# Reordering the first loads of a block-sparse attention and bilinear feed-forward kernel

## The chip, the cores and the metric

The kernel runs on one core of one Trainium2 chip. The metric is device time in microseconds (us), from the start of the program to its end, as the median of several runs; lower is better. One execution more is profiled, and all rows below come from that one.

## The reference

Attention over 4 batches, 8 heads, 768 positions and head size 64, with a block mask (24 blocks of 32), followed by a bilinear feed-forward (3072 tokens, 512 to 1536 to 512):

```python
scores = scale * np.matmul(q, k.transpose(0, 1, 3, 2))
mask = np.abs(blk_i - blk_j) <= 1
mask = mask | (blk_i == 0) | (blk_j == 0) | (blk_i == 23) | (blk_j == 23)
for qb in range(24):
    for kb in sampled_blocks[qb]:            # three random blocks a row
        mask[qb*32:(qb+1)*32, kb*32:(kb+1)*32] = True
scores = np.where(mask, scores, -1e9)
attn = np.exp(scores - max); attn = attn / (sum + 1e-9)
x = np.matmul(attn, v)                       # to (B*S, H*D)
out = ((x @ w_a) * (x @ w_b)) @ w_out
```

Each block row attends to at most eight blocks (itself, its neighbours, the first, the last and three sampled ones); block rows 0 and 23 attend to all.

## The kernel before

**Tiling.** A chunk is 256 queries, so there are three chunks per batch and twelve in all. They are worked in the order 1, 2, 0, 3 and so on (`seq`). A chunk has eight block rows, called blocks here and numbered n in working order. For a sparse block, GpSimd (POOL) copies its keys out of `keysT` into `KG` (lines 774 to 782), SP loads its value rows into `VG` (lines 809 to 827), TensorE writes the mask and the scores into the PSUM tile `s` (`all_scores`), VectorE takes the row maximum (line 1151), ScalarE the exponential (line 1161), and after normalizing and transposing (lines 1047 and 1054, or a DMA transpose) TensorE sums the values into `av` (line 1074), from which ScalarE and VectorE make `xT`. Batch 0 keys and the first two chunks' values are used as float32 (`plain`); later ones are split into two float16 parts.

**Weights.** The 36 weight tiles (12 each of w_a, w_b, w_out) come as 64-bit numbers on POOL's DMA queue (`weights`, line 914). VectorE makes float32 of each with three instructions (lines 935, 938, 941), then each is bounded, scaled and split into two float16 halves. The feed-forward's first products (`ab`, line 1422) need these and a whole chunk of `xT`; its second ones (`o`, lines 1525 to 1527) follow.

**Tables.** `make_tables` loads five small arrays: the sampled blocks three times in different layouts, the row offsets `c_rows` and the block table `c_blocks`. From them VectorE makes the address tables (`offs`, `offs_k`, `rows_at`: `starts`, lines 520 to 533) and then the mask rows `mrows` and the selecting matrix `ident` (`doubles`, lines 542 to 558). Every sparse block's scores need `mrows`, and every gather of keys or values needs the address tables.

**The order.** No engine's instruction order is written out by hand. The program is a set of generators ("flows"); a planner in the kernel, run when the program is built, gives each requested step a cost in ns and issues next the one that can begin first by those costs, with the flow's rank as a small weight and as the tie-breaker (lower rank first):

```python
best = min(asked, key=lambda a: (a[0] + weigh[a[3].eng] * a[1], a[1]))
```

Ranks are block numbers: a flow with rank 16 stands with the work of block 16. The planner also models eight DMA completion lanes (`LANES = 8`): a transfer can be issued only when the one eight earlier has landed. Ahead of the real pass it tries 500 random changes of the ranks (fixed seed) and keeps those that bring its own end no later. So each cost and each rank that is changed can change the order of instructions anywhere in the program; on the chip, each engine then works strictly through the order that it was given, waiting by semaphores.

Names that matter below: `make_tables`, `make_eye` (loads the 128 by 128 unit matrix that the transposes use), `queries_plain`, `keys_plain` (four loads, one per two heads, on ScalarE's DMA queue, each started from the one before), `weights`, `bound_values` (batch 0's values, 1.5 MB, on POOL's queue, line 634).

Of the kernel before, what the change touches and what calls it, by code (L numbers as in the profile page):

```python
# [61 lines left out]
LEAD_K, LEAD_V, LEAD_Q, LEAD_X, LEAD_G = 10, 9, 8, -1, 2  # L62
GATE_KV, GATE_Q, GATE_G = 10, 10, 4
EARLY_K, EARLY_V, APART = 21, 14, 2
R_W, R_W_STEP = 16, 0.05
FIRST_W = 3
LATE_W, R_V0 = 9, 8
W_PE, W_DVE, W_ACT, W_POOL, W_SP = 0, 1, 0, 0, 2
# [176 lines left out]
Way = namedtuple("Way", "eng ns fn moved extra", defaults=(0, 0))  # L245
# [6 lines left out]
def dve(ns, fn):  # L252
    return [Way("DVE", ns, fn)]
# [10 lines left out]
def load_way(moved, fn):  # L264

    return [Way("LOAD", 475, fn, moved)]
# [7 lines left out]
def sp(ns, moved, fn):  # L274
    return [Way("SP", ns, fn, moved)]
# [72 lines left out]
def program(nc, plan, pools, q, k, v, sampled_blocks, w_a, w_b, w_out, c_blocks, c_ident, c_rows, out):  # L348
# [27 lines left out]
    def take(tag, bufs):  # L376
        return rings.setdefault(tag, Ring(bufs)).take()
# [109 lines left out]
    def make_tables():  # L487

        box = work.tile([P, DM], F32, tag="st", name="mbox", bufs=ST_BUFS)
        held = yield from take("st", ST_BUFS)  # L490
        row = work.tile([P, DM], F32, tag="st", name="mrow", bufs=ST_BUFS)
        held2 = yield from take("st", ST_BUFS)
        sb = box[:NB, 0 : 2 * NR].bitcast(I32).rearrange("p (a b) -> p a b", b=2)
        cb = box[:NB, 8 : 8 + 5 + NB]
        sv = box[:NB, 40:48]
        eq = box[:NB, 48:56]
        dup = box[:NB, 56:64]
        one = row[0:1, 0 : 2 * NR * NB].bitcast(I32).rearrange("p (a b) -> p a b", b=2)
        clamped = row[0:1, 256 : 256 + NR * NB]
        clamped3 = clamped.rearrange("p (b a) -> p a b", b=NR)  # L500
        seen = box[: NR * BLK, 64 : 64 + 2 * NB].bitcast(I32).rearrange("p (a b) -> p a b", b=2)
        within = box[: NR * BLK, 120:121]
        words = sampled_blocks.bitcast(I32)

        def load():
            nc.sync.dma_start(
                one.rearrange("p (r a) b -> p r (a b)", r=NR),
                words.rearrange("(o r x) a -> o r x a", o=1, x=BLK)[:, :, 0],
            )
            nc.sync.dma_start(  # L510
                sb, words.rearrange("(r x) (a w) -> x a r w", x=BLK, w=2)[0]
            )
            nc.sync.dma_start(seen.rearrange("p a b -> p (a b)"), words)
            nc.sync.dma_start(within, c_rows)
            nc.sync.dma_start(cb, c_blocks)

        yield [Way("SP", 1400, load, 250, 1)]

        def starts():
            nc.vector.tensor_scalar(  # L520
                clamped, one[:, :, 0], 0.0, float(NB - 1), ALU.max, ALU.min
            )
            rows = box[: NR * BLK, 128 : 128 + NB]
            nc.vector.tensor_scalar(
                rows, seen[:, :, 0], 0.0, float(NB - 1), ALU.max, ALU.min
            )
            nc.vector.tensor_scalar(
                rows_at, rows, float(BLK), within, ALU.mult, ALU.add
            )
            nc.vector.tensor_scalar(  # L530
                offs[:, :, :NR], clamped3, float(BLK), None, ALU.mult
            )
            nc.vector.tensor_scalar(
                offs_k[:, :, :NR], clamped3, float(BLK // 2), None, ALU.mult
            )

        t = yield dve(1050, starts)
        tables.fire(t)
        held2.fire(t)

        def doubles():
            nc.vector.tensor_copy(sv[:, 0:5], cb[:, 0:5])
            nc.vector.tensor_scalar(
                sv[:, 5:8], sb[:, :, 0], 0.0, float(NB - 1), ALU.max, ALU.min
            )
            nc.vector.memset(ident, 0.0)
            nc.vector.memset(mrows, 0.0)
            nc.vector.tensor_copy(ident[:NB], cb[:, 5 : 5 + NB])
            nc.vector.memset(dup, 0.0)
            at = (0, 1, 2, 3, 7, 4, 5, 6)  # L550
            for s in range(3, 8):
                nc.vector.tensor_scalar(
                    eq[:, :s], sv[:, :s], sv[:, s : s + 1], MASKED, ALU.is_equal, ALU.mult
                )
                nc.vector.tensor_reduce(
                    dup[:, at[s] : at[s] + 1], eq[:, :s], axis=mybir.AxisListType.X, op=ALU.min
                )
            nc.vector.tensor_copy(mrows[:NB], dup.unsqueeze(2).to_broadcast([NB, 8, BLK]))  # L558

        t = yield dve(2300, doubles)  # L560
        held.fire(t)
        mask_ready.fire(t)


    def make_eye():
        gone = yield from take("hl", HL_BUFS)
        t = yield sp(650, 200, lambda: nc.sync.dma_start(eye, c_ident))
        id_ready.fire(t)
        yield eye_used
        gone.fire(eye_used.at)  # L570
# [21 lines left out]
    def keys_plain(g):  # L592
        t = yield load_way(1500, lambda: nc.scalar.dma_start(keys32[:, g], k[0, g]))
        k_ready[0].fire(t)
        if g + 1 < NG:
            plan.start(keys_plain(g + 1), -LEAD_K)
        else:
            plan.start(queries_plain(seq[1]), order[0, seq[1] * PER] - LEAD_Q)
            plan.start(weights(0), R_W)
# [5 lines left out]
    def queries_plain(cc):  # L605
        u0 = order[0, cc * PER]
        yield from gate(u0 - GATE_Q)
        used = yield from take("QT", QT_BUFS)
        q_used[cc] = used
        QT[cc] = QTs[place[cc] % QT_BUFS]  # L610
        t = QT[cc].rearrange("p a h x -> p (a h x)").bitcast(F32)
        if place[cc] < QT_BUFS:
            nc.gpsimd.memset(t[D:, : H // 2 * CH], 0.0)
            nc.gpsimd.memset(t[:D, H // 2 * CH :], 0.0)

        def load():
            nc.sync.dma_start(t[:D, : H // 2 * CH], q0[cc][:D])
            nc.sync.dma_start(t[D:, H // 2 * CH :], q0[cc][D:])

        t = yield [Way("SP", 1100, load, 1700, 1)]  # L620
        q_ready[cc].fire(t)
        n = place[cc] + 1
        if n == NCH:
            b1, c1 = divmod(seq[n], NCH)
            plan.start(queries(seq[n]), order[b1, c1 * PER] - LEAD_Q)
        elif n > 1:
            plan.start(queries_plain(seq[n]), order[0, seq[n] * PER] - LEAD_Q)
# [37 lines left out]
    def keys(b, g):  # L665
        yield from gate(first_of[b] - (GATE_KV if b < 2 else EARLY_K - APART * g))
        raw, freed = yield from raw_tile(b, g, 0)
        yield pool_load(1000, 1000, lambda: nc.gpsimd.dma_start(raw, k[b, g]))
        t = yield LATE_LOAD
        if g + 1 < NG:  # L670
            plan.start(keys(b, g + 1), first_of[b] - LEAD_K, t - APART_LOADS if b == 1 else 0.0)
        elif b > 0:
            plan.start(values(b, 0), first_of[b] - LEAD_V)
        t = raw.rearrange("p (t d) -> p t d", d=D)
        done = yield from take("ks", KS_BUFS)
        ks = work.tile([P, 2 * NT, P], F16, tag="ks", name=f"ks{b}_{g}", bufs=KS_BUFS)
        at = at_k + b * NG + g
        s = scale[:, at : at + 1]
        yield act(1020, lambda: nc.scalar.activation(
            ks[:, :, :D], t, AF.Abs, accum_out=bound[:, at : at + 1]  # L680
        ))
        end = yield from set_scale(slice(at, at + 1), FLOOR_QK)
        k_scale[b].fire(end)
        yield act(930, lambda: nc.scalar.activation(ks[:, :, :D], t, AF.Copy, scale=s))
        end = yield dve(1070, lambda: nc.vector.scalar_tensor_tensor(
            ks[:, :, D:], t, s, ks[:, :, :D], ALU.mult, ALU.subtract
        ))
        freed.fire(end)
        if b == 1:
            yield w_freed  # L690
        if b >= 2:
            yield k_free[b - 2]
        end = yield sp(1700, 2200, lambda: nc.sync.dma_start_transpose(
            keysT[b % 2][:, 2 * g : 2 * g + 2, :].rearrange("p h (t s) -> p (h t) s", s=P),
            ks.rearrange("p t d -> p (t d)"),
        ))
        done.fire(end)
        k_ready[b].fire(end + LATE_LOAD)
# [851 lines left out]
    nc.vector.memset(bound, 0.0)  # L1550
    nc.scalar.activation(warm, warm, AF.Exp)
    nc.vector.memset(cq[:, :NCH], float(D) ** -0.5)
    plan.start(make_tables(), -LEAD_K - 1)
    plan.start(queries_plain(seq[0]), -LEAD_K - 1)
    plan.start(keys_plain(0), -LEAD_K)
    plan.start(make_eye(), -LEAD_K)
    plan.start(keys(1, 0), first_of[1] - LEAD_K)
    plan.start(gather_keys(0), -LEAD_G)
    plan.start(gather_values(0), -LEAD_G)
# [80 lines left out]
```

## Time and profile before

| | |
|---|---|
| median of 3 runs | 844.45 us (838.79 to 862.81) |
| the profiled execution's own time | 842.29 us |
| its span, first to last instruction | 840.5 us |
| TensorE busy | 778.7 us (93%) |
| VectorE / ScalarE / POOL busy | 579.7 / 528.9 / 255.2 us |
| mean granted TensorE clock | 0.984 of full |
| first matmul begins | 18.60 us |

The table is read so: TensorE has work for 93% of the span, so the end can only move by the 62 us in which it has none, or by the stretches in which it is slow. The granted clock is given in parts of 2.4 GHz; 0.50 is 1.2 GHz.

### The profile page before, as it was taken

The page shows a single profiled execution, that of the slowest core. Times are in us where ns is not written, and L with a number is a line of the kernel's source. Part 1 is how long each engine was busy: PE and PEld are TensorE (multiplying, and loading weights), DVE is VectorE, ACT ScalarE, POOL GpSimd, SP SyncE. Part 2 cuts the span into 40 slices and gives each one's busy share as a digit, 9 for nine tenths or more (in the row PEclk, how much of TensorE's full clock was granted, in tenths as well). Part 3 has the DMA queues.
Part 4 walks back from the last instruction along what each step waited for, and adds up shares of the span by engine and source line. Part 5 has one row for each costly group of instructions (what it writes and reads, how often), then busy time and mean ns, then how long its engine had stood idle before and what let it go on. Part 6 is the DMA issues. An engine that isn't in the chain of part 4 may idle for free.

```text
span 840.5 us, 24045 instructions
## 1 busy us (share of the span) xinstructions
PE 778.7 (93%) x8952; PEld 577.9 (69%) x8952; DVE 579.7 (69%) x1690; ACT 528.9 (63%) x1429; POOL 255.2 (30%) x561
## 2 busy tenths in 40 slices
PE   1788898999996999999989999999899999999997
PEld 0566676785783578886766777777677768776743
DVE  3899999997775989757668797667767644222242
ACT  0788877888665777656667776656666444434342
POOL 5676237633163654103433340034232000000000
PEclk9699999999998999999999999999999999999999
DMA  8886878986679999977999886846765542300001
GB/s 281 244 281 215 251 183 238 256 209 123 171 131 142 244 239 196 189 156 170 170 214 192 191 208 160 191 132 150 157 134 120 148 109 50 89 2 27 1 26 50
DMA packets 179410, 135.22 MB, mean 161 GB/s; under 512 B 127102, under 2 KB 148734, under 8 KB 179294
## 3 DMA queue, kind: packets, MB, share of 16 engines
q1 hardware_dynamic: 167182, 89.26, 50.6%
q0 software_dynamic: 11536, 42.87, 17.8%
q8 instruction: 70, 1.15, 0.6%
q10 hardware_dynamic: 576, 1.57, 0.6%
q14 instruction: 46, 0.38, 0.2%
HBM read 91.71 MB, written 12.58 MB: 124 GB/s over the span
## 4 chain that ended last, share of the span: by engine, by line
PE 66%; DVE 16%; DMA 6%; ACT 6%; issue 5%; POOL 1%; POOLq 0%; SPq 0%; ACTq 0%; DVEq 0%
PE ab L1422 35%; PE av L1074 7%; PE o L1525 6%; PE o L1526 6%; PE o L1527 6%; PE s L1007 3%; DMA pt<-hl 2%; DVE low L1151 1%; DVE xT L1390 1%; PE s L1136 1%; DVE hl L1032 1%; ACT sm L1161 1%; DMA q<-in_q_dram 1%; DVE wab L938 1%; DVE wab L961 1%
## 5 line engine op out<-in xcount | busy, mean ns | idle before, releaser
L1422 PE MATMUL ab<-xT,wab 128*128 128x256 f16 x3456 | 397.4, 274 | 7.3 <-ACT pt L1180 2.8
L1422 PEld LDWEIGHTS <-wab 128*128 128x128 f16 x3456 | 333.4, 98 | 61.5 <-issue 20.4
L474 POOL PARTITION_ALL_REDUCE power<-bound x70 | 32.9, 471 | 322.5 <-DVE bound L1474 197.1
L1074 PE MATMUL av<-pt,VG 128*128 128x64 f16 (+1 forms) x2544 | 120.4, 204 | 10.5 <-issue 7.2
L1161 ACT ACTIVATE sm<-s,low,cq 128x256 f32<-128x256 f32 x176 | 97.7, 557 | 48.5 <-DVE hl L1032 28.1
L1497 DVE SCALAR_TENSOR_TENSOR gl<-a,gto,gh 128x256 f16<-128x256 f32 x144 | 70.5, 492 | 74.3 <-ACT gh L1490 73.8
L1490 ACT ACTIVATE gh<-a,gto 128x256 f16<-128x256 f32 x144 | 71.8, 503 | 76.2 <-PE o L1526 72.8
L1525 PE MATMUL o<-woh,gh 128*128 128x512 f16 x288 | 110.1, 382 | 4.9 <-DVE ou L1542 4.6
L1526 PE MATMUL o<-wol,gh 128*128 128x512 f16 x288 | 109.9, 381 | 0.0
L1527 PE MATMUL o<-woh,gl 128*128 128x512 f16 x288 | 109.9, 381 | 0.0
L1454 ACT ACTIVATE a<-ab,f 128x256 f32<-128x256 f32 x144 | 67.4, 468 | 64.5 <-PE ab L1422 42.4
L1457 DVE TENSOR_TENSOR a<-a,ab 128x256 f32<-128x256 f32 x144 | 60.0, 416 | 66.5 <-ACT a L1454 65.6
L780 POOL COPY KG<-keysT 128x128 int32 x264 | 93.6, 391 | 35.2 <-POOL KG L775 21.7
L1074 PEld LDWEIGHTS <-VG 128*128 128x128 f16 x2256 | 78.1, 98 | 21.2 <-issue 13.6
L775 POOL COPY KG<-keysT 128x384 int32<-128x384 int32 x88 | 53.8, 611 | 124.7 <-PE s L1007 104.5
L1032 DVE SCALAR_TENSOR_TENSOR hl<-sm,den,hl 128x256 f16<-128x256 f32 (+1 forms) x174 | 88.3, 511 | 3.9 <-ACT hl L1025 2.2
L1460 ACT ACTIVATE ga<-a 128x256 f16<-128x256 f32 x144 | 59.4, 413 | 30.5 <-DVE a L1457 28.9
L1151 DVE TENSOR_REDUCE low<-s 128x2 f32<-128x512 f32 x88 | 59.9, 681 | 15.2 <-PE s L1007 13.3
L1136 PE MATMUL s<-mrows,ident 128*32 128x192 bf16 (+1 forms) x352 | 25.0, 273 | 32.0 <-DVE mrows L558 18.6
L1527 PEld LDWEIGHTS <-gl 128*128 128x128 f16 x288 | 28.3, 98 | 34.6 <-issue 0.8
L1028 DVE TENSOR_SCALAR hl<-sm,den 128x256 f16<-128x256 f32 (+1 forms) x119 | 43.8, 369 | 11.7 <-DMA pt<-hl 11.5
L1526 PEld LDWEIGHTS <-gh 128*128 128x128 f16 x288 | 28.3, 98 | 33.4 <-issue 6.6
(126 smaller groups left out, 975.5 us busy)
## 6 DMA issues: line engine op xcount, KB each, us to landing
VG<-vd SPq DMA_DIRECT2D x73, 192.0 KB, 3.7
VG<-vd SPq DMA_DIRECT2D x189, 64.0 KB, 2.4
VG<-vd SPq DMA_DIRECT2D x28, 384.0 KB, 4.2
q<-in_q_dram POOLq DMA_DIRECT2D x36, 256.0 KB, 4.9
keysT<-in_moe_w_out_dram POOLq DMA_DIRECT2D x12, 512.0 KB, 4.7
out_dram<-ou SPq DMA_DIRECT2D x24, 256.0 KB, 2.1
stage<-in_k_dram POOLq DMA_DIRECT2D x12, 384.0 KB, 6.4
stage<-in_v_dram POOLq DMA_DIRECT2D x12, 384.0 KB, 5.2
```

Source lines behind the costliest of these rows:

```text
L780: nc.gpsimd.tensor_copy(to[:, :, (4 + r) * w : (5 + r) * w], of[:, :, bass.ds(at, w)])
L1032: t = yield dve(221 + n * 1.03, lambda: nc.vector.scalar_tensor_tensor(lo, sm, over, hi, ALU.mult, ALU.subtract))
L1074: mm(av[:, g, i % 2, :], w, pt[:, y, cols], start=(i % 2 == 0 and g == 0 and first and n + m == 0), stop=(last and n == len(terms) - 1 and ...
L1151: yield dve(685, lambda: nc.vector.tensor_reduce(mx, ps, axis=mybir.AxisListType.X, op=ALU.max, negate=True))
L1161: t = yield act(750, lambda hq=hq: nc.scalar.activation(sm[:, hq], ps[:, hq], AF.Exp, bias=low[:, at, hq, 0:1], scale=cq[:, cc, hq : hq + ...
L1422: mm(ab[:, i, :], wab[:, f, i, part, kt, :], xc[:, kt, a, :], start=(i == 0 and kt == 0 and part + a == 0), stop=(kt == KT - 1 and a == 1) ...
L1454: yield act(470, lambda: nc.scalar.activation(a_sb, ab[:, 0, :], AF.Copy, scale=fb[:, f : f + 1]))
L1490: yield act(400, lambda: nc.scalar.activation(gh, a_sb, AF.Copy, scale=s))
L1497: t = yield dve(485, lambda: nc.vector.scalar_tensor_tensor(gl, a_sb, s, gh, ALU.mult, ALU.subtract))
L1525: mm(po, gh[:, js], woh[:, f, :], start=(f == 0), stop=False)
L1526: mm(po, gh[:, js], wol[:, f, :], start=False, stop=False)
L1527: mm(po, gl[:, js], woh[:, f, :], start=False, stop=(f == NF - 1))
```

## The change

The table loads get the lowest rank, so that they are issued first; keys get rank -14, in front of queries at -11; the unit matrix gets -4, behind both. The weights' rank goes from 16 to 14. Three costs that the planner assumes change too: the tables' loads 700 ns instead of 1400, the address tables 1150 instead of 1050, the mask rows 4800 instead of 2300. No instruction is added or removed; the change acts through the order alone.

```diff
-R_W, R_W_STEP = 16, 0.05
+R_W, R_W_STEP = 14, 0.05
...
-        yield [Way("SP", 1400, load, 250, 1)]
+        yield [Way("SP", 700, load, 250, 1)]
...
-        t = yield dve(1050, starts)
+        t = yield dve(1150, starts)
...
-        t = yield dve(2300, doubles)
+        t = yield dve(4800, doubles)
...
-            plan.start(keys_plain(g + 1), -LEAD_K)
+            plan.start(keys_plain(g + 1), -LEAD_K - 4)
...
-    plan.start(make_tables(), -LEAD_K - 1)
+    plan.start(make_tables(), -LEAD_K - 8)
     plan.start(queries_plain(seq[0]), -LEAD_K - 1)
-    plan.start(keys_plain(0), -LEAD_K)
-    plan.start(make_eye(), -LEAD_K)
+    plan.start(keys_plain(0), -LEAD_K - 4)
+    plan.start(make_eye(), -LEAD_K + 6)
```

(`LEAD_K` is 10.)

## Rows read from the trace of the kernel before

**Rows 1.** Busy time by stretch: start:end us, length, engines, clock, DMA share, GB/s
```profile
0.00:18.60 18.60, 0.00 (x0) 0.10 (x1) 5.39 (x26) 1.49 (x2) 10.41 (x25) 1.00 0.86 273
18.60:40.00 21.40, 16.01 (x124) 10.98 (x123) 18.55 (x49) 14.98 (x34) 12.35 (x25) 0.68 0.84 252
40.00:100.00 60.00, 50.81 (x547) 38.31 (x547) 58.83 (x164) 51.06 (x135) 37.22 (x68) 1.00 0.83 256
100.00:160.00 60.00, 56.24 (x610) 44.83 (x609) 56.96 (x170) 47.59 (x123) 29.55 (x50) 0.97 0.84 223
160.00:240.00 80.00, 77.59 (x836) 57.26 (x834) 68.05 (x206) 63.10 (x169) 27.25 (x58) 1.00 0.67 163
240.00:280.00 40.00, 32.77 (x442) 22.29 (x440) 26.36 (x81) 23.05 (x64) 21.92 (x48) 0.91 1.18 172
```

**Rows 2.** Waits of TensorE over the whole span: total us, times, longest
```profile
PE s L1136 <- DVE mrows L558: 18.6, 1, 18.6
PE s L1136 <- ACT sm L1161: 13.4, 8, 4.1
PE av L1074 <- issue: 7.2, 1, 7.2
```

**Rows 3.** Chain that ended last, its first pieces: start us, us, what
```profile
1.39 5.83 DMA QT<-in_q_dram
...
7.23 6.05 DMA mbox<-c_rows
```

**Rows 4.** Timeline of SP's queue: start us, us to issue
```profile
2.64 0.82 SPq L506 DMA_DIRECT2D mrow<-in_sampled_blocks_dram  x1
...
8.19 0.30 SPq L515 DMA_DIRECT2D mbox<-c_blocks  x1
```

**Rows 5.** Timeline of VectorE: start us, us, [idle before <- releaser]
```profile
13.38 0.23 DVE L527 TENSOR_SCALAR rows_at<-mbox 96x24 int32<-96x24 f32 x1 [3.34 <-DMA mbox<-c_rows]
...
18.27 0.28 DVE L558 CAST mrows<-mbox 24x256 bf16<-24x256 f32 x1
18.47 0.41 DVE L935 TENSOR_SCALAR wab<-stage 128x512 int32<-128x512 int32 x1
```

**Rows 6.** Waits of SP's queue, first 40 us
```profile
SPq L514 <- DMA QT<-in_q_dram: 2.1, 1, 2.1
```

**Rows 7.** Timeline of POOL
```profile
4.59 0.69 POOL L914 DMA_DIRECT2D stage<-in_moe_w_a_dram  x1
...
13.58 0.88 POOL L634 DMA_DIRECT2D wab<-in_v_dram  x1 [7.21 <-DMA mbox<-c_blocks]
14.45 0.52 POOL L775 COPY KG<-keysT 128x384 int32<-128x384 int32 x1
...
16.07 0.52 POOL L775 COPY KG<-keysT 128x384 int32<-128x384 int32 x1
```

**Rows 8.** The fourth key load (line 593), start 6.19, and its landing
```profile
L593 ACTq DMA_DIRECT2D keysT<-in_k_dram x1: 334/334/334, 6.2 to 6.2; - x1
DMA to landing us min/median/max: 6.8/6.8/6.8
```

**Rows 9.** DMA issues by form: count, KB each, median us to landing
```profile
stage<-in_moe_w_a_dram POOLq DMA_DIRECT2D x4, 512.0 KB, 7.6
...
wab<-in_v_dram POOLq DMA_DIRECT2D x1, 1536.0 KB, 8.6
```

**Rows 10.** DMA issues of the whole span: the quickest form
```profile
out_dram<-ou SPq DMA_DIRECT2D x24, 256.0 KB, 2.1
```

**Rows 11.** Busy time by stretch around TensorE's first wait, columns as in group 1
```profile
22.00:26.00 4.00, 0.12 (x4) 0.09 (x1) 3.71 (x9) 2.35 (x8) 3.61 (x8) 0.87 1.04 276
26.00:32.00 6.00, 4.49 (x31) 2.84 (x30) 4.77 (x15) 6.00 (x14) 3.13 (x7) 0.50 0.44 113
32.00:39.00 7.00, 7.00 (x46) 5.37 (x46) 5.70 (x17) 4.93 (x12) 3.65 (x8) 0.53 0.92 314
```

**Rows 12.** Timeline of all engines: the first transposes, which read the unit matrix
```profile
28.23 1.12 PE L1054 MATMUL tp<-eye,sm 128*128 128x128 f32 x4
```

## The prediction

> **What bounds the kernel now.** I read the busy time by stretch first. It shows three stages [rows 1]. Up to 18.60 us TensorE does nothing. From there to 100 us VectorE is the full engine (18.55 of 21.4 us, then 58.83 of 60), while TensorE has 16.01 and 50.81; to 160 us both are nearly full. Behind that TensorE sets the pace, with 2.4 us idle from 160 to 240 and 7.2 from 240 to 280. Over the whole span it is idle for 62 us; it was busy for 123.1 up to 160, so for 655.6 of the 680.5 behind, and 25 of the idle time lie there. So a gain at the start counts if the VectorE stage as a whole slides forward, and it is kept by the TensorE stage behind it, which has no slack to absorb it.
>
> The waits of TensorE come next [rows 2]: by far the longest single one is the first, 18.6 us, for the mask rows `mrows`. The chain of waits says why they are late [rows 3]: a query transfer that lands at 7.2 us, and then the row offsets `c_rows`, issued at 7.23 and on their way for 6.05 us. SP's queue shows the same from its side: it held the fourth table load for 2.1 us until a query transfer had landed [rows 6], so the five table loads, whose issues cost 0.82 us at the first and 0.30 at the last (2.16 in all five), are strung out from 2.64 to 8.49 [rows 4]. VectorE then needs from 13.38 to 18.55 for address tables and mask, 5.17 us, and starts on the weights at 18.47 [rows 5].
>
> The third look is at what would be late next. POOL's timeline has a wait of 7.21 us for `c_blocks` in front of the load of batch 0's values at 13.58 [rows 7]; that load does not read `c_blocks`, so I read it as the lane rule of the code (eight transfers on). Behind it in POOL's order stand the first key copies, 14.45 to 16.07. The last keys were there at about 13.0 (6.19 + 6.8) [rows 8]. The copies for one block take 1.62 us, and from the mask's end at 18.55 to the first matmul it was 0.05. So without the mask the first scores could begin at about 16.1 already in the present order, and at about 14.7 if POOL were free when the keys land (13.0 + 1.62 + 0.05).
>
> **The change, part by part.**
>
> *Tables first.* SP issues them from 0.74 (where the first query load stands now) to about 2.9, all on fresh lanes, so the waits for query and key landings go. Their landing in an otherwise quiet first three microseconds is not in the trace. From below I bound it by 2.1 us, the quickest form of the whole span [rows 10], from above by 6.05, the same kind of load in full traffic [rows 3]. I take 4, between them: keys start beside them but weights do not (POOL issues none before 4.59 [rows 7]). Tables at 6.9, mask 5.17 later at 12.1, with ends 10.2 and 14.1. In each case that is ahead of the first key copies' end (14.6), so the mask leaves the path, and keys plus copies are next.
>
> *Queries and unit matrix behind.* The queries go 2.2 us later through SP's queue, and perhaps some more for lanes; the second half landed at 7.2 [rows 3], so 9.4 to 12, still before the key copies are done: nothing. The unit matrix is read by the transposes at 28.23 first [rows 12]; 20 us of cover: nothing. If both covers failed the price would be the delay itself, at most 3 us.
>
> *Keys ahead of queries.* They are issued by ScalarE's queue and so do not stand behind SP's work; the fourth waited until 6.19, and with its lane taken by a table that lands early it can go some 3 us sooner. What it gains depends on the traffic, which was at a share of 0.86 from 0 to 18.6 us [rows 1]. From below (all 3 us gained): first scores at 11.7. From above (nothing gained, POOL not freed either): 16.1. I take 14.7, unchanged landing with POOL free, which is nearest to the row as it stands. Against 18.6 that is 3.9 us sooner, with ends 2.5 and 6.9.
>
> *The weights' start.* The first weight tile was issued at 4.59 and needed about 7.6 us [rows 7, 9], so it was there at about 12.2; VectorE began it at 18.47 because the mask was in front. With the mask done at 12.1 it begins 6.3 us sooner.
>
> The VectorE stage therefore slides by something between 3.9 (its attention part) and 6.3 (its weights part). I take 4.5, nearer to the scores because the first maximum needs them.
>
> *Rank 14 for weights.* Where block 14 or 15 and a weight tile could both begin, the weight now goes first. TensorE idles 9.2 us from 40 to 100 [rows 1]; if weights are what it lacks, up to all of that comes back, if attention is what it lacks, as much again is lost. Both are in the same stretch, so I take 0 and keep both ends.
>
> *The new costs.* 4800 is close to what VectorE takes (4.7 of the 5.17 us); they act through the order alone. Every order after them can differ. What a different order can do behind 160 us is bounded by TensorE's 25 idle us there, of which 7.2 are one stop in the middle of a value sum that waits for no semaphore [rows 2]. I take 0, with 5 us each way.
>
> Sum: 842.3 (the profiled time; span 840.5 and 1.8 around it) - 4.5 = 837.8, so **838 us**. The profiled execution is 2.2 us under the median of the three runs, which differ by more than the whole effect.
>
> **Rivals.**
>
> *A. The start is bound by traffic, not by order (842 us).* With its lane free, the load of values, 1536 KB [rows 9], would be issued at about 6.5 instead of 13.58, beside keys, queries and weights. At the 273 GB/s of the first 18.6 us [rows 1] these bytes take 5.8 us. If they all come ahead of the last keys, these land at 18.8 and not 13.0, and the first scores at 20.5, so that what the tables gain is lost; with half of them ahead it is 17.6 and nothing measurable. Against it: POOL's queue holds three weight tiles of 512 KB in front of the values, and the keys are all queued before those. The Trainium skill, "DMA: Bandwidth & Descriptors", section "Issuing engines are not separate DMA queues", says that transfers from any engine end up on the same 16 DMA engines and interleave, which would give this rival. The trace agrees so far as a row bears on it: a share of 0.86 while SP, ScalarE and POOL all had loads on their way [rows 1, 4, 7, 8].
>
> *B. The first gap closes too (828 us).* After its first two blocks TensorE waited 4.1 us for the exponential [rows 2], because VectorE's order had weights ahead of the first maximum; the clock then fell to 0.50 (1.2 GHz) and was still there for most of 32 to 39 us (0.53 on average) [rows 11]. In 26 to 39 TensorE was busy for 11.5 us; at full clock that is up to 5.7 us less. With a cost for the mask near the true one the order may fit better: 4.1 + 5.7 on top of 4.5 gives 842.3 - 14.3 = 828. Against it: VectorE is the full engine there and gets no faster by TensorE's clock. The Trainium skill's "TensorE: Matmul & The Clock Gate", section "HAM oscillation — how this bites in real kernels", has the same pattern of a wait that costs clock behind it; the trace agrees, 0.50 after the 4.1 us wait.
>
> *C. Weights in front starve TensorE (853 us).* If blocks 14 and 15 are pushed back behind weight tiles, the chunk that they complete comes later, and TensorE has neither scores nor first products. The idle 9.2 us of 40 to 100 double, and a wait as long as that of 4.1 us brings one more stretch at half clock, 5.7 us: 842.3 - 4.5 + 9.2 + 5.7 = 852.7. It decides from the point where the added idle time passes the 4.5 us. For it: VectorE is full, so whatever is put first takes from the other. Against it: only the last two of sixteen blocks change places, and TensorE was not idle for lack of these.
>
> *D. The order does not change as described.* The random search moves ranks by up to 2 a step; the new gaps (-18, -14, -11, -4) are wider than that, so tables not coming first is unlikely. It would give 842, and I count it with A.
>
> **How the numbers follow.** Forecast 0.50 (834 to 842), A and D 0.20 (839 to 847), C 0.17 (846 to 860), B 0.13 (823 to 832). The predicted time is the forecast's, 838. To leave out 2 in 10, I cut B's lower part and C's upper part: 827 to 851, which takes in the 5 us of reordering behind 160. Two per cent, about what a measurement of this kernel can tell from no change, is 17 us: faster by that means under 827.6, slower over 861.3. The first needs B and some more: 0.09. The second needs C at its top or a worse order: 0.05. Within: 0.86.
>
> **What would show it.** In the changed profile: table loads at SP from about 0.7 to 3 us with no wait between them; `mrows` done at 10 to 14; POOL's value load no longer behind `c_blocks`; first scores at 12 to 16, released by key copies and no longer by `mrows`; the first weight conversion at 11 to 13; the same total busy times. Rival A shows in a fourth key load that lands later than 13; B in a clock that stays at 1.00 from 26 to 39; C in more than 10 us of idle TensorE from 40 to 100. The prediction is wrong if the sum of TensorE's idle time behind 160 us moves by more than 5 from its 25, for then the order, and not the start, decides.

## The result, and the profile after

The changed kernel took 845.8 us (median of 6 runs, 843.65 to 865.51) against 841.6 for the kernel before on the same chip. The ratio is 1.011, with a 95% interval of 1.006 to 1.016: slower by about 9 us by that ratio, where a gain of 4.5 was forecast. The medians are over all runs; the ratio leaves out, on both sides, the runs more than 1.5% above the fastest of their kernel. The time lies inside the predicted range; the sign does not. The profiled execution took 850.56 us, the longest of the runs that the ratio counts.

The busy time by stretch of the kernel after answers to [rows 1]; columns are the same, and the last row is a stretch read by itself.

```profile
0.00:18.60 18.60, 2.23 (x27) 1.14 (x30) 5.15 (x27) 1.49 (x2) 8.68 (x22) 1.00 0.75 200
18.60:40.00 21.40, 15.76 (x190) 10.40 (x182) 15.47 (x44) 14.97 (x38) 13.44 (x34) 1.00 1.01 287
40.00:100.00 60.00, 54.30 (x466) 41.83 (x467) 53.02 (x147) 46.40 (x119) 28.63 (x56) 0.80 0.79 239
100.00:160.00 60.00, 53.78 (x491) 43.28 (x489) 55.88 (x165) 47.83 (x121) 25.89 (x45) 0.94 0.66 202
160.00:240.00 80.00, 75.55 (x831) 50.87 (x829) 72.76 (x214) 63.47 (x167) 35.09 (x62) 1.00 0.88 191
...
40.00:66.00 26.00, 22.56 (x145) 15.96 (x146) 19.23 (x55) 16.37 (x45) 13.08 (x25) 0.54 0.89 253
```

Three things differ. TensorE has work ahead of 18.60 us, as forecast. VectorE, which was full from 18.6 to 100 (18.55 and 58.83 us), now is not: 15.47 and 53.02. And TensorE's 54.30 us in 40 to 100 are not more work but slower work: 466 matmuls against 547, at a clock of 0.80, with 0.54 from 40 to 66. A count of matmuls is rough, since they differ in length; by these rows the kernel after is 93 ahead at 40 us (217 against 124), about level at 100 (683 and 671), and runs 491 against 610 from 100 to 160. Over the whole span TensorE's idle time is the same (61.8 us before, 61.7 after) and its busy time is longer (778.7 to 787.0). Of the 8.2 us by which the two profiled spans differ, 5.2 are work that TensorE still has to do at 160 us (660.9 us against 655.7, at a clock of 0.99 in both), and 3.0 are idle time behind it. So most of the loss comes ahead of 160 us. The clock row alone would blame the clock; the experiments show that it is not enough to read.

The waits of TensorE over the whole span answer to [rows 2], and the timeline of TensorE shows its first work and its first long gap.

```profile
PE s L1136 <- DVE mrows L558: 9.0, 1, 9.0
...
PE s L999 <- POOL KG L780: 8.2, 2, 7.4
```

```profile
16.72 1.93 PE L999 MATMUL s<-KG,QT 128*32 128x256 f32 x16 [7.38 <-POOL KG L780]
...
42.73 0.35 PE L1136 MATMUL s<-mrows,ident 128*32 128x192 bf16 x4 [1.94 <-ACT sm L1161]
```

The mask left the path, at 9.0 instead of 18.6. The first scores then waited for POOL's key copies until 16.72, so 1.9 us were gained, not 3.9. SP's queue [rows 4] and VectorE [rows 5] show the tables first, without the wait of [rows 6], and the mask rows done at 8.9; VectorE's timeline goes on to what is new:

```profile
0.75 0.88 SPq L506 DMA_DIRECT2D mrow<-in_sampled_blocks_dram  x1
...
2.97 0.40 SPq L515 DMA_DIRECT2D mbox<-c_blocks  x1
...
6.41 0.42 SPq L820 DMA_DIRECT2D VG<-in_v_dram  x1
```

```profile
8.65 0.28 DVE L558 CAST mrows<-mbox 24x256 bf16<-24x256 f32 x1
14.08 0.43 DVE L935 TENSOR_SCALAR wab<-stage 128x512 int32<-128x512 int32 x1 [5.14 <-DMA stage<-in_moe_w_a_dram]
...
22.91 0.42 DVE L935 TENSOR_SCALAR wab<-stage 128x512 int32<-128x512 int32 x1
...
26.19 0.42 DVE L935 TENSOR_SCALAR wab<-stage 128x512 int32<-128x512 int32 x1
...
37.80 0.43 DVE L935 TENSOR_SCALAR wab<-keysT 128x512 int32<-128x512 int32 x1 [4.11 <-DMA keysT<-in_moe_w_b_dram]
```

Each L935 opens one weight tile. Before, the first four began at 18.47, 19.52, 21.07 and 28.97; now at 14.08, 22.91, 26.19 and 37.80. Only the first came sooner. At the fourth VectorE stands for 4.11 us, and behind it in its queue stand the reciprocal, the row maximum and the normalizing step of attention (38.15 to 39.94), and TensorE has work for 2.3 of the 7 us from 36 to 43. The chain of waits, which began with a query transfer and `c_rows` before [rows 3], now runs through a weight load, the sixth, that lands at 43.61 as VectorE takes it up at 43.63:

```profile
35.17 8.44 DMA keysT<-in_moe_w_b_dram
```

The reason is on POOL, the answer to [rows 7]:

```profile
4.60 0.68 POOL L914 DMA_DIRECT2D stage<-in_moe_w_a_dram  x1
14.52 0.50 POOL L775 COPY KG<-keysT 128x384 int32<-128x384 int32 x1 [9.24 <-DMA VG<-in_v_dram]
...
18.24 0.56 POOL L914 DMA_DIRECT2D stage<-in_moe_w_b_dram  x1
...
20.59 0.53 POOL L914 DMA_DIRECT2D stage<-in_moe_w_a_dram  x1
...
22.92 0.88 POOL L634 DMA_DIRECT2D wab<-in_v_dram  x1 [0.56 <-issue]
...
29.36 0.56 POOL L914 DMA_DIRECT2D keysT<-in_moe_w_b_dram  x1
```

Before, three weight loads (4.59, 5.29, 5.82) and the value load (13.58) stood ahead of the first key copies, and the fourth weight load went at 17.75. Now one stands ahead; the others wait behind copies that wait for the keys. (The row puts the wait of these copies down to a value gather; it landed at 14.47, the fourth key load at 14.3, and which of the two the copies needed last is not shown.) Ahead of the fifth load, at 34.65, POOL stands for another 4.73 us with nothing that the profile shows to wait for. The fourth key load is late itself, the answer to [rows 8]: start 5.5, landing 8.8 us later, at 14.3 and not 13.0.

```profile
L593 ACTq DMA_DIRECT2D keysT<-in_k_dram x1: 334/334/334, 5.5 to 5.5; - x1
DMA to landing us min/median/max: 8.8/8.8/8.8
```

### The profile page after: what moved, and what is told of

Its sections match the earlier page's. It is cut to its first block, busy times and chain, and to the rows that moved or that the text cites. A ratio compares the mean times of both kernels' runs of the same rounds, so it can differ in the third digit from the quotient of the medians.

```text
span 848.7 us, 24053 instructions
## 1 busy us (share of the span) xinstructions
PE 787.0 (93%) x8952; PEld 583.3 (69%) x8952; DVE 579.4 (68%) x1687; ACT 531.4 (63%) x1432; POOL 250.1 (29%) x561
## 3 DMA queue, kind: packets, MB, share of 16 engines
q0 software_dynamic: 11536, 42.87, 17.8%
## 4 chain that ended last, share of the span: by engine, by line
PE 55%; DVE 15%; DMA 11%; ACT 7%; issue 5%; POOL 3%; SPq 2%; POOLq 1%; ACTq 0%; DVEq 0%
PE ab L1422 28%; DMA pt<-hl 6%; PE av L1074 6%; PE o L1525 6%; PE o L1527 5%; PE o L1526 5%; PE s L1007 3%; DVE hl L1032 2%; ACT sm L1161 1%; DVE low L1151 1%; DVE xT L1390 1%; POOL KG L780 1%; DMA q<-in_q_dram 1%; POOLq L751 1%; DMA keysT<-in_moe_w_b_dram 1%
## 5 line engine op out<-in xcount | busy, mean ns | idle before, releaser
L1074 PE MATMUL av<-pt,VG 128*128 128x64 f16 (+1 forms) x2544 | 125.6, 207 | 14.9 <-DMA pt<-hl 5.6
L474 POOL PARTITION_ALL_REDUCE power<-bound x70 | 37.3, 533 | 330.9 <-DVE bound L1474 184.8
L780 POOL COPY KG<-keysT 128x128 int32 x264 | 87.3, 367 | 32.7 <-POOL KG L775 23.0
L775 POOL COPY KG<-keysT 128x384 int32<-128x384 int32 x88 | 49.5, 563 | 135.8 <-PE s L1007 109.7
L1525 PEld LDWEIGHTS <-gh 128*128 128x128 f16 x288 | 28.1, 98 | 33.0 <-issue 5.3
L1526 PEld LDWEIGHTS <-gh 128*128 128x128 f16 x288 | 28.2, 98 | 31.4 <-issue 4.6
```

Source lines behind the costliest of these rows:

```text
L780: nc.gpsimd.tensor_copy(to[:, :, (4 + r) * w : (5 + r) * w], of[:, :, bass.ds(at, w)])
L1074: mm(av[:, g, i % 2, :], w, pt[:, y, cols], start=(i % 2 == 0 and g == 0 and first and n + m == 0), stop=(last and n == len(terms) - 1 and ...
L1525: mm(po, gh[:, js], woh[:, f, :], start=(f == 0), stop=False)
L1526: mm(po, gh[:, js], wol[:, f, :], start=False, stop=False)
```

## The experiments

The theory: the change's harm is POOL's order of loads, which starves VectorE of weights, and not the tables. Rivals: the tables-first start itself; the rank of the weights as such; the order behind 160 us; the clock. In every comparison below the kernel before ran beside the others on the same chip.

**One part alone (e1, e3, e4).** e1 takes the kernel before and lets SP issue the five table loads first; every other engine keeps its order.

```diff
-        yield [Way("SP", 1400, load, 250, 1)]
+        load()
+        yield [Way("SP", 1400, lambda: None, 250, 1)]
```

> The kernel before with one thing changed: the five table loads stand first in SP's order; the order of every other engine, and the planner's search, stay as they were. Theory P (the forecast's step: the start bounds, and its gain is kept): mask done near 9 us, first scores at 14.5 to 15, ratio to the kernel before 0.993 to 0.997 (836 to 839 us). Rival L (what follows is bound by the loads that POOL issues, so an earlier start is only waited away): ratio 0.998 to 1.002. Rival T (tables first are themselves the harm in the changed kernel): 1.005 or more.

Measured: 840.7 us (13 runs) against 838.0, ratio 1.0014 [0.9966, 1.0062]: nothing. This is what rival L gave. The profiled execution took 872 us, far above the median, and only its rows up to 64 us are used. POOL's wait ahead of the value load did not go with `c_blocks`; another transfer took its place, and the key copies began at 16.55, the first scores at 18.28. POOL's and VectorE's timelines:

```profile
15.68 0.88 POOL L635 DMA_DIRECT2D wab<-in_v_dram  x1 [9.31 <-DMA VG<-in_v_dram]
16.55 0.52 POOL L776 COPY KG<-keysT 128x384 int32<-128x384 int32 x1
```

```profile
16.31 3.85 DVE L939 SCALAR_TENSOR_TENSOR wab<-stage,wab 128x512 int32<-128x512 int32 x1
```

VectorE's lead from the early first weights went too: an instruction that takes 0.69 us elsewhere took 3.85 while POOL's copies ran from 16.55 to 20.3.

e4 changes only the rank of the weights.

```diff
-R_W, R_W_STEP = 16, 0.05
+R_W, R_W_STEP = 14, 0.05
```

> The kernel before with the rank of the weights at 14 and nothing else; the search runs anew on it, and POOL's order comes out with key copies ahead of the second weight load. Theory L (any edit that loses the searched order loses the early loads): ratio 1.005 to 1.02, though no table load moved. Rival (rank 14 starves TensorE in 40 to 100 us by putting weights ahead of blocks 14 and 15, as rival C of the prediction): 1.01 to 1.02 with the added idle time at 70 to 110 us. Rival (rank 14 harmless and the order too): 0.997 to 1.003.

Measured: 846.4 us, 1.011 [1.004, 1.018], the same as the whole change. Its order has all that the change's order has: tables first (mask at 9.0), one weight load ahead of the key copies, first scores at 16.76, 7.5 us of VectorE waiting for weights from 18.6 to 64. The sign of the rival with rank 14, more idle time of TensorE from 70 to 110 us, is all but missing (4.4 us before, 5.2 in e4). So the trace speaks against the place of the weights before blocks 14 and 15, and for the new order that the planner makes. e3 gets such an order with the rank left at 16, by leaving out the random search and nothing else:

```diff
-ROUNDS, SHARE, REACH, SEED = 500, 0.05, 2.0, 0
+ROUNDS, SHARE, REACH, SEED = 0, 0.05, 2.0, 0
```

> The kernel before without the planner's search over ranks (no rounds); ranks and costs as before. Its order on POOL has one weight load, then key copies, then the other loads, as in the changed kernel, and the tables late. Theory L: slower than the kernel before, ratio 1.008 to 1.025 (849 to 863 us), VectorE starved behind 30 us. Rival (the search's ranks are worth nothing on the chip, and the harm is the tables or rank 14): ratio 0.995 to 1.005.

Measured: 853.4 us, 1.021 [1.015, 1.028]. POOL's head is again one weight load, then key copies, and the tables are first (both expectations had them late). The planner gives that head (one weight load ahead of the key copies, tables first) to ten versions whose orders were read, most of them without a run: before without its search and with three other seeds, the rank of the weights alone, the tables' rank alone, and after, as it is, without search and with two other seeds. The three costs alone keep the head of the kernel before, three loads and the values ahead of the copies and the tables behind the queries. So that head is a find of one seed of the search, and not every edit loses it.

**The loads put back (e2).** The kernel after, with the second and third weight load and the value load issued ahead of the first key copies on POOL.

```diff
         def copies():
+            if n == 0:
+                for m in (1, 2):
+                    weight_load(m)
+                values_load()
             nc.gpsimd.tensor_copy(to[:, :, 0 : 3 * w], ...)
```

(`weight_load` and `values_load` issue a load once; their definitions are left out here.)

> The changed kernel with one thing changed: the second and third weight loads and the load of batch 0's values stand ahead of the first key copies in POOL's order, as they do in the kernel before; all other engines keep the changed kernel's order. Theory L (these loads behind key copies starve VectorE at 34 to 44 us, and the clock falls behind that): VectorE's waits of 4.1 and 2.4 us go, no stretch at half clock from 43 to 65 us, ratio to the kernel before 0.985 to 0.998 (829 to 840 us). Rival R (the order elsewhere in the program is worse): ratio 1.005 to 1.015, as the changed kernel. Rival V (values beside the keys delay these, as rival A of the prediction): fourth key later than 15 us and a ratio near 1.00.

Measured: 859.2 us, 1.024 [1.017, 1.032]: slower still, so the time that the theory gave for it was wrong. Its step was right: VectorE waited for no weights from 18.6 to 64, and the clock was 0.92 from 43 to 65 (0.50 in the kernel after). The time was lost elsewhere, as rival R had it, though by more than R gave. Busy time from 240 to 340 us of the kernel before, then of e2:

```profile
240.00:340.00 100.00, 90.82 (x1243) 66.79 (x1241) 79.26 (x234) 72.41 (x195) 52.52 (x114) 0.97 1.10 199
```

```profile
240.00:340.00 100.00, 83.20 (x1074) 60.09 (x1072) 66.00 (x201) 62.68 (x169) 44.25 (x95) 0.93 1.08 174
```

16.8 us without work for TensorE in this stretch, 9.2 even in the kernel before. SP's queue shows what stands there: DMA transposes, of the keys of batch 2 (`keysT<-ks`) and of attention rows (`pt<-hl`). Before:

```profile
242.85 1.24 SPq L1214 DMA_TRANSPOSE pt<-hl  x1
...
246.40 5.45 SPq L693 DMA_TRANSPOSE keysT<-ks  x1
251.96 12.43 SPq L1214 DMA_TRANSPOSE pt<-hl  x2
264.43 0.58 SPq L820 DMA_DIRECT2D VG<-vd  x1
```

An issue of 1.24 us becomes one of 12.43 for two behind a key transpose, and the value gathers behind it on SP wait as long. In e2, from 240 to 340, the longest such pair took 12.77, and the longest key transpose 9.93 itself.

**The same four orders without that stage (f1 to f4).** The key transposes of batches 2 and 3 become plain copies of the same bytes; everything else runs.

```diff
-        end = yield sp(1700, 2200, lambda: nc.sync.dma_start_transpose(
+        end = yield sp(1700, 2200, lambda: (nc.sync.dma_start_transpose if b < 2 else nc.sync.dma_start)(
```

> The kernel before, but the keys of batches 2 and 3 are moved into their tile by a plain copy of the same bytes in place of the DMA transpose, so their scores are those of other numbers; nothing else changes, in no engine's order. Theory S (the stage from 240 to 340 us is paced by SP's DMA queue, where the four key transposes of batch 2 hold up the transposes of the probabilities): TensorE's idle time between 240 and 340 us falls from 9 us to under 4, SP's longest issue of a probability transpose there from 12.4 us to under 4; ratio to the kernel before 0.975 to 0.99. Rival (the stop of 7.2 us was code loading or chance): ratio 0.995 to 1.003.

> As the run before it, with the five table loads first in SP's order as well. In the experiment with the tables alone, TensorE's work was 6.8 us ahead of the kernel before from 40 to 160 us, and the end was not. Theory S (the lead is lost in the stage of the key transposes): with these gone the end is 4 to 8 us sooner than f1_before_copy_keys, a ratio to the kernel before lower than its by 0.005 to 0.010. Rival R (the lead is lost for another reason): within 0.003 of it.

> The changed kernel with the same plain copy of keys. It was 5.6 us of TensorE work behind the kernel before at 240 us. Theory S: that lag, from the stretch of 40 to 120 us, is now what stands between the two: slower than f1_before_copy_keys by 4 to 9 us (0.005 to 0.011). Rival (what it loses, it loses in the stage of the transposes): within 0.003 of f1_before_copy_keys.

> The changed kernel with the POOL loads ahead of the first key copies and the same plain copy of keys. It was 5.3 us ahead of the kernel before in TensorE's work from 100 to 240 us, and then lost 12 us from 280 to 320. Theory S: faster than f3_after_copy_keys by 6 to 12 us and than f1_before_copy_keys by 2 to 6. Rival R (its order later in the program is a bad one): slower than f1_before_copy_keys by 5 us or more, as its ratio of 1.024 was.

Measured, as ratios to the unchanged kernel before (839.8 us): f1 (before) 0.993 [0.988, 0.998]; f2 (tables first) 0.988 [0.978, 0.998]; f3 (after) 1.000 [0.996, 1.005]; f4 (after, loads ahead) 0.987 [0.979, 0.996]. In f1's profile TensorE's idle time from 240 to 340 fell from 9.2 us to 2.2 and the stop of 7.2 us is gone, as theory S said; the time fell less than S gave. Whether the tables first help (f2 against f1) can't be told within these intervals.

The kernel after without the transposes is 0.7% slower than the kernel before without them (f3 to f1; 837.9 and 832.0 by the medians). Putting the loads back is worth 1.3% by the ratios (f3 to f4) and 0.6% by the medians of all runs (837.9 and 833.2), with the sign that e2 lacked. The two profiles do not show that step: f3's is its second quickest execution of eleven (832.2, with 2.6 us of waits for weights), f4's took 834.1, and the eighth weight tile begins at 52.33 in the one and 52.15 in the other.

By the ratios, which come from different chips, the transposes cost the kernel before 0.7%, the kernel after 1.1% and e2 3.7%; so most of e2's loss lies there. From 240 to 340 in f4's profile:

```profile
240.00:340.00 100.00, 98.09 (x1376) 75.31 (x1375) 82.21 (x249) 78.85 (x216) 53.26 (x120) 1.00 0.91 206
```

**POOL's order alone (g1 to g4).** The cleanest cut: the kernel before, all orders as they are, with the second and third weight load and the value load moved behind the key copies of the first two blocks (g1; g2 with copied keys), and e1 with the value load alone moved so (g3; g4 with copied keys).

```diff
                     to[:, :, (4 + r) * w : (5 + r) * w], of[:, :, bass.ds(at, w)]
                 )
+            if n == 1:
+                for m in (1, 2):
+                    weight_load(m)
+                values_load()
```

> The kernel before, with nothing changed but three of POOL's DMA issues: the second and third weight load and the value load are issued behind the key copies of the first two blocks instead of ahead of them, as POOL has them in the kernel after. Everything else keeps the order of before, the tables last included. Theory S (POOL's load order in the first 25 us is the harm of the change): VectorE has only one weight block to convert by 25 us, waits on weights between 25 and 45, and the ratio is 1.007 to 1.02, some 846 us. Theory T (the harm lies in the order behind, that the planner makes after the first 25 us): the ratio is 0.997 to 1.003, whatever VectorE waits for early.

> The same edit of POOL's order in the kernel before whose key transposes of batches 2 and 3 are plain copies of the same bytes (the right keys of those batches are left out). Without the edit that kernel's ratio was 0.993 [0.988, 0.998]. Theory S: 0.998 to 1.005, 5 to 8 us above that. Theory T: 0.993 again.

> The kernel before with the five table loads first on SP, and the value load on POOL behind the key copies of the first two blocks; the three weight loads stay ahead of them. In the run with the tables first alone, POOL stood 9.3 us at the value load and the key copies began at 16.6. Theory V (that wait alone took the forecast gain): key copies at 13 to 14, first scores at 14.5 to 16, and 2 to 4 us of it last to the end, ratio 0.995 to 0.998. Rival M (POOL's wait only moves on again, to the key copies, whose semaphores count the same loads): key copies at 15 to 17 and a ratio of 1.000 to 1.004. Rival W (the start is sooner and what TensorE gains is taken up by 100 us, or the values come late for the first second products): ratio 1.000 with TensorE 3 to 4 us ahead at 40 us in its profile and not at 160.

> The same order as the run before this, with the key transposes of batches 2 and 3 as plain copies of the same bytes (the right keys of those batches are left out). With the tables first alone this gave 0.988 [0.978, 0.998]. Theory V: 0.982 to 0.986. Rivals M and W: 0.987 to 0.993.

Measured: g1 1.006 [1.000, 1.013]; g2 1.002 [0.999, 1.006]; g3 1.004 [0.999, 1.008]; g4 0.998 [0.992, 1.003]. Between g2 and f1, whose only difference is that order, lie 0.9% by the ratios, with intervals that just do not meet: theory S. The two ran on different chips, each beside its own kernel before; by the medians of all runs (832.0 against 839.8, and 838.4 against 843.3) the step is 0.35%. So its sign is shown, and its size lies somewhere between 0.35 and 0.9%. g1 alone would not have told S from T, since its interval touches 1.000. V did not come true. Of its rivals the profile bears out M, in g3 by the time too: the key copies began at 15.5 and 15.7, in g4 when the last keys landed (15.5). g4's time is above what all three gave, for its value load, moved behind, took the fourth weight load with it (19.3 in f2, 22.1 here). That load also takes longer right behind the 1.5 MB of values: 10.6 us to landing in g2, and in g4 VectorE takes it up 12.0 us after its issue, against 8.4 in f2. So the bytes in front count beside the place in the queue.

Where f1 and g2 part is seen on POOL and VectorE. f1 first, then g2:

```profile
18.80 0.54 POOL L914 DMA_DIRECT2D keysT<-in_moe_w_b_dram  x1
...
28.71 0.42 DVE L935 TENSOR_SCALAR wab<-keysT 128x512 int32<-128x512 int32 x1
...
45.76 0.42 DVE L935 TENSOR_SCALAR wab<-stage 128x512 int32<-128x512 int32 x1
```

```profile
16.97 0.55 POOL L920 DMA_DIRECT2D stage<-in_moe_w_b_dram  x1
...
23.11 0.54 POOL L920 DMA_DIRECT2D keysT<-in_moe_w_b_dram  x1 [0.77 <-issue]
```

```profile
21.15 0.43 DVE L958 TENSOR_SCALAR wab<-stage 128x512 int32<-128x512 int32 x1 [4.52 <-DMA stage<-in_moe_w_b_dram]
...
33.70 0.43 DVE L958 TENSOR_SCALAR wab<-keysT 128x512 int32<-128x512 int32 x1 [3.03 <-DMA keysT<-in_moe_w_b_dram]
...
51.74 0.52 DVE L958 TENSOR_SCALAR wab<-stage 128x512 int32<-128x512 int32 x1
```

```profile
15.62 0.35 PE L1159 MATMUL s<-mrows,ident 128*32 128x192 bf16 x4 [15.62 <-DVE mrows L558]
...
27.86 0.35 PE L1159 MATMUL s<-mrows,ident 128*32 128x192 bf16 x4 [8.31 <-ACT sm L1184]
...
35.98 3.68 PE L1097 MATMUL av<-pt,VG 128*128 128x64 f32 x16 [5.07 <-ACT pt L1203]
```

g2 begins TensorE's work 2.8 us sooner than f1 and has lost 7.8 us by 64: TensorE busy 29.36 us against 37.19 from 18.6 to 64, VectorE 35.41 against 41.87. VectorE stands for 7.5 us at weights; less the 2.8 us by which it began its first tile sooner (15.50 and 18.28), that is about the 5.0 us by which the fourth tile is later (28.71 and 33.70). The seventh is 6.0 us later (45.76 and 51.74), and the spans end 5.8 apart (830.1 and 835.9): what VectorE loses here lasts to the end.

All kernels side by side; the waits for weights are VectorE's, those that end between 18.6 and 64 us.

| | first scores, us | 4th weight load, us | waits for weights, us | ratio |
|---|---|---|---|---|
| before | 18.7 | 17.8 | 0 | 1 |
| e1 | 18.3 | 20.3 | 0 | 1.001 |
| e2 | 17.9 | 30.9 | 0 | 1.024 |
| after | 16.7 | 29.4 | 6.5 | 1.011 |
| e4 | 16.8 | 27.1 | 7.5 | 1.011 |
| e3 | 17.2 | 29.2 | 6.2 | 1.021 |
| g1 | 16.0 | 21.9 | 7.1 | 1.006 |
| g3 | 18.2 | 21.7 | 6.2 | 1.004 |
| *copied keys:* f1 | 18.5 | 18.8 | 0 | 0.993 |
| f2 | 17.4 | 19.3 | 0.3 | 0.988 |
| f4 | 17.8 | 30.8 | 1.0 | 0.987 |
| f3 | 15.7 | 28.7 | 2.6 | 1.000 |
| g2 | 15.7 | 23.1 | 7.5 | 1.002 |
| g4 | 18.5 | 22.1 | 7.3 | 0.998 |

Among the six with copied keys the three without waits of note lie at 0.987 to 0.993 and the three with them at 0.998 to 1.002. The first scores do not sort them: the two soonest are among the slow. Before and f1, after and f3, e1 and f2, e2 and f4, g1 and g2, g3 and g4 are the same program up to 240 us, so each pair is two executions of one order: the orders with and without waits stay apart, but the size can differ (6.5 us in after, 2.6 in f3). With real keys e2 falls out of the pattern, by the transposes. No version that computes all of the output beat the kernel before.

## Why the prediction was wrong, point by point

That the time lies in the range is owed to the width that the rivals gave it, not to the mechanism.

*Tables first.* The mask was done at 8.9, ahead of the low end of 10.2: the tables were there at about 5.5, not 6.9, and VectorE took 3.4 us to the mask's end, not 5.17. The step was right, and the mask left the path.

*First scores "at about 14.7 if POOL were free when the keys land (13.0 + 1.62 + 0.05)".* This term failed: 16.72, a gain of 1.9. POOL was free, since its value load had moved behind; but the keys were not there at 13.0, and the copies of the first block took 2.1 us instead of 1.62. In the two profiles of the change's early order the keys landed at 14.3 and 13.2, with the loads put back at 15.2 (f4), in before's order with the tables first at 13.8 (f2) and 15.5 (g4), against 13.0 and 10.6 for before and f1. Before and f1 have one order, so 2.4 us of this is scatter, but all five lie above both. That is rival A's sign, the late fourth key load, though not by its mechanism: the 1.5 MB value load went at 22.92. From 5 to 10 us eight of the ten tables-first kernels moved 245 to 286 GB/s (e2 311, f4 328), and the four others 305 to 339, with value gathers on SP from 6.41 in the kernel after instead of 9.10. Whether those gathers hold up the keys was not tried.

*"The first weight tile ... begins 6.3 us sooner."* It began 4.4 us sooner. But the VectorE stage does not slide by its first tile. The second, third and fourth began 3.4, 5.1 and 8.8 us later, for their loads stood behind the key copies on POOL. I took POOL's order of loads as given, although the ranks of keys and weights had been edited, both ahead of it in the list. **This is the step that failed:** that the VectorE stage slides forward with its first inputs, because POOL's loads stay where they were.

*"Rank 14": 0, ± 9.2.* The price came, by another road: of the first ten weight tiles all but the first began later than before (the tenth at 67.28 instead of 58.82), so none was put in front of a block. Rival C had weights in front starving TensorE; what came was weights behind starving VectorE, and with it TensorE. C's mark, over 10 us of idle TensorE from 40 to 100, did not show (5.7), because TensorE ran at 0.80 there and so looked busy. C's other sign, one more stretch at half clock behind a wait, did come, from 43 to 65 (0.50).

*"The new costs": 0, with 5 us each way.* What a new order can do was undersized, and it is not symmetric. The order before was the best of a search; the three versions in which the planner made another one and that were run are all slower, and e3, which only leaves the search out, costs 2.1%, some 18 us. For such a kernel zero is not the middle of what a new order can do. The costs by themselves were not run.

*Rival D*, that the order changes otherwise than described, I counted as "tables not coming first is unlikely". They come first; what changed beside was POOL. *Rival B* was half right: the clock did stay at 1.00 from 26 to 39, and then fell from 40 to 66. Its reading of the rows before does not hold, though: the sixteen score matmuls took 1.94 us at 18.71, ahead of the 4.1 us wait, as at 26.35 behind it, and 1.04 from 40 on. So TensorE was slow from its first matmul, and the rows do not show that the wait cost clock.

*"A gain at the start counts"*, as the TensorE stage keeps it: true of losses (g2 against f1), but a sooner first score is not such a gain. In g1 and g2 it came 2.8 us sooner and the loss was there at once, as VectorE sets the pace from 18.6 to 100. The mark "wrong if the idle time behind 160 us moves by more than 5" was not passed: 24.8 to 27.8.

What stays open: why e2's order meets the key transposes so much worse than before's, and how much of the change's 1.1% lies there; by f1 and f3 it is 0.7% without them, and the rest is within the intervals. That POOL's order of loads costs time is shown by g2 against f1 and, by the medians alone, by f3 against f4; that it is all of the 0.7% is not shown, for f3's one profile has no more work left at 160 us than f1's (653.0 and 654.7). What the stretch at half clock costs by itself was not tried.

## What to carry to other kernels

Where a planner with a search writes the order, compare the issue order of every queue before costing an edit, and price a new draw by a run without the search. Where one engine is full behind a gap, ask for its later inputs as well as for the first: a sooner start is worth nothing if its next loads stand behind the work that was brought forward. A stage that looks busy at a low clock is not read from its busy time: compare the length of one and the same group of matmuls, and the work that is left behind the stage.

## What the runs showed of the hardware

A VectorE instruction with two inputs in SBUF stretched from 0.69 to 3.85 us beside twelve key copies on POOL, in e1 and f2. The Trainium skill, "SBUF — State Buffer", section "Who interferes with whom", says that such an instruction contends with GpSimd instructions that read SBUF; the trace agrees, and shows in these two runs a wait as long as the whole train of copies (16.55 to 20.3 in e1). It is not always so: beside key copies the same kind of instruction took at most 1.20 us in the kernel after and 0.99 in g3.

A DMA transpose issue on SP took 1.24 us alone and up to 12.43 for two behind a key transpose.

The granted clock of a profile can miss a slow stretch. Before and f1 are the same program up to 240 us; the rows give 0.50 from 26 to 32 us for the one [rows 11] and 1.00 throughout 20 to 60 for the other. But the same sixteen matmuls took the same 3.68 us in both, against 2.00 behind 40 us. The kernel before, then f1:

```profile
30.61 3.68 PE L1074 MATMUL av<-pt,VG 128*128 128x64 f32 x16 [1.27 <-ACT pt L1180]
```

```profile
30.36 3.68 PE L1074 MATMUL av<-pt,VG 128*128 128x64 f32 x16 [1.28 <-DMA QT<-in_q_dram]
...
40.73 2.00 PE L1074 MATMUL av<-pt,VG 128*128 128x64 f32 x16
```

So TensorE was equally slow in both. In the kernel after, such a group took 2.00 us at 25.55 and 3.68 at 44.72, where the granted clock says 1.00 and 0.50: there the two agree.

What does differ between executions of one order is when loads land. In after and f3, which are the same program up to 240 us, VectorE begins the fourth weight tile at 37.80 and 35.28 and the seventh at 48.23 and 44.63. So one profile can differ from another of the same program by 3.6 us, which is why the verdicts here rest on medians and ratios of many runs.
